# Attention and an ELU MLP on one core: the swapped copy of q by DMA, exp(h) - 1 on ScalarE, and q, k and the last weights of a pair handled at other half slots

## The chip, the cores and the metric

The kernel runs on one core of one Trainium2 chip. The metric is device time in microseconds of one execution; lower is better. Three runs of the kernel before gave 1304.9, 1305.69 and 1305.71 us, so the median is 1305.69 us. The engines are named as in the profile: PE (TensorE), ACT (ScalarE), DVE (VectorE), POOL (GpSimd) and SP, whose queue issues every DMA of this kernel.

## What is computed

The reference is RMS-normalised attention for 8 batches of 12 heads (448 positions, 64 wide), then an MLP whose activation is ELU with alpha = 1:

```python
q_n, k_n = rmsnorm(q, g_q), rmsnorm(k, g_k)
scores = (1 / np.sqrt(64)) * q_n @ k_n.transpose(0, 1, 3, 2)
attn = np.exp(scores - max) ; attn = attn / (sum(attn) + 1e-9)
x = (attn @ v) -> (8 * 448, 768)
h = x @ w_in                                  # 768 -> 2048
g = np.where(h > 0, h, np.exp(np.minimum(h, 0)) - 1)
out = g @ w_out                               # 2048 -> 768
```

Matmuls run on float16 parts: every operand is split into a high and a low float16 part, and a product of two operands is three matmuls (high by high, high by low, low by high) that add up in PSUM. For q and k, the high and the low part of one head share the 128 partitions.

## The kernel before, in words

**Tiles.** Two heads form a pair `p` (48 pairs, 6 per batch). The scores of a pair are 896 rows of 448, handled as 7 chunks `T` of 128 rows; `T % NJ` (NJ = 7) is the chunk's place in its pair. The MLP of a batch is 16 groups `f` of 18 matmuls (the m1 part, `w_in`, tile `mo`) and then 6 groups `d` of 48 matmuls (the m2 part, `w_out`).

**Half slots.** The order on every engine is written out by hand. One loop runs over half slots `h`; two half slots are one chunk and 14 are one pair. In each half slot the loop records the chunk's steps, then the tasks that `at(h, fn)` has put down for `h`, then a share of the MLP's matmuls (576 per 84 half slots, from h = 92 on), then the scores of the next chunk. Engines run their own instructions in this order, each waiting only for the data and the buffers that it needs.

**A chunk.** `s_mm` makes the scores on PE into one of four PSUM banks `s`. `s_max` (DVE) takes the row maximum, `s_exp` (ACT) the exponential and its sum, `s_z` (POOL) adds 1e-9, `s_rec` (DVE) takes the reciprocal, `s_hi` (ACT) writes the high part of the weights, `s_lo` (DVE) the low part, after which the bank is free. `s_tr` transposes both parts by a DMA into the tiles `pt` of the two heads. In chunk numbers: `s_max` of T stands at h = 2T, `s_exp` at 2T + 1, `s_z` and `s_rec` at 2T + 2 and 2T + 3, `s_hi` and `s_lo` at 2T + 4 and 2T + 5, and `s_tr` at 2T + 6 (2T + 8 for the first chunk of a pair, since its tile `pt` is free only after `attend` of the pair before).

**A pair.** `attend(p)` (22 matmuls on PE into the bank `av`) stands at h = 14(p + 1) + 7, and `x_high` (ACT) and `x_low` (DVE) bring its result into the MLP's input. Ahead of a pair, with hb = 14(p - 1), its q and k are prepared: `load_qk`, `qk_square` (ACT), `qk_sum` (DVE), `qk_root` (ACT), `qk_newton` (DVE), `qk_norm` (POOL, line 391), `k_high` (ACT), `q_gain` (POOL for pairs 1 to 6, otherwise DVE, line 405), `q_high` (ACT), `k_low` and `q_low` (POOL, lines 414 and 421), the two `qk_transpose` (DMAs, line 429) and `q_swap` (line 436). `q_swap` writes a copy of the transposed q whose two halves of 64 partitions have changed places; `s_mm` needs it for the second of its two matmuls, so that low parts meet high parts.

**The first batch.** Up to h = 92 there is attention alone on PE; beside it run the conversion of `w_in` (16 slabs, `conv_in`, with `s_high` on POOL at line 282) and later of `w_out` (24 slabs, `conv_out`, POOL at lines 313 and 322). From h = 92 on the MLP of one batch runs beside the attention of the next one. For v, POOL does `v_mult`, `v_high`, `v_low` and `v_shift` (lines 440, 448, 453, 459).

**A group of m1.** `m1_out` has five steps, one per half slot after the group's last matmul: exp(h) on ACT (line 614), minus 1 and times a power of two on POOL (617), the choice between that and h on DVE (623), and the high and low parts of g on ACT (628) and DVE (631).

Of the kernel before, what the change touches and what calls it, by code (L numbers as in the profile page):

```python
# [13 lines left out]
AF = mybir.ActivationFunctionType  # L14
ALU = mybir.AluOpType
# [7 lines left out]
NC_, NF = DM // 128, DFF // 128  # L23
NJ = 2 * S // 128
# [8 lines left out]
def tile_attention_then_elu_mlp(ctx: ExitStack, tc: tile.TileContext, qk, v, v_scan, gg, w_in, w_out, out):  # L33
# [13 lines left out]
    nc = tc.nc  # L47
# [15 lines left out]
    def t_mo():  # L63
# [8 lines left out]
        out=neg, in0=ident, scalar1=-1.0, scalar2=None, op0=ALU.mult  # L72
# [43 lines left out]
    def small(name, w=1, dt=F32, bufs=2):  # L116
        return pool.tile([128, w], dt, tag=name, name=name, bufs=bufs)
# [19 lines left out]
    def ibits(dst, src, s1, op0, s2, op1):  # L137
        nc.vector.tensor_scalar(
            out=dst.bitcast(I32), in0=src.bitcast(I32), scalar1=s1, scalar2=s2, op0=op0, op1=op1
        )  # L140
# [195 lines left out]
    vscale, mscale, vpow = {}, {}, {}  # L336
# [96 lines left out]
    def q_swap(p):  # L433
        q = qkt[p]
        for a, z in ((64, 0), (0, 64)):
            nc.gpsimd.tensor_copy(out=q[z : z + 64, 2], in_=q[a : a + 64, 0])  # L436

    def v_mult(p):
        n = vn[p]
# [49 lines left out]
    def m_scale(b):  # L489

        p2 = vpow[b]
        if b == 0:
            ibits(a_in, a_in, POWER, ALU.bitwise_and, 0, ALU.bitwise_or)
        am = small("am")
        nc.vector.tensor_reduce(out=am, in_=a_in, axis=AX.X, op=ALU.max)
        sc, isc = small("sc", NF), small("isc", NF)
        gsc = small("gsc", NF)
        nc.vector.tensor_scalar(  # L500
            out=sc, in0=a_in, scalar1=p2, scalar2=2.0 ** (-28 - UP), op0=ALU.mult, op1=ALU.mult
        )
        ibits(isc, sc, -1, ALU.mult, 254 * E, ALU.add)

        u = small("u", bufs=3)
        nc.vector.tensor_scalar(
            out=u, in0=am, scalar1=p2, scalar2=2.0 ** (-12 - UP), op0=ALU.mult, op1=ALU.mult
        )
        ui = small("ui")
        ibits(ui, u, -1, ALU.mult, 254 * E, ALU.add)  # L510
        nc.vector.tensor_scalar(out=gsc, in0=sc, scalar1=ui, scalar2=None, op0=ALU.mult)
        mscale[b] = [sc, isc, gsc, u]

    def cuts(j):

# [50 lines left out]
    def s_lo(T):  # L566

        p16, ps, r = p16s[T], pss.pop(T), stats.pop(T)[:, 2:3]
        nc.vector.scalar_tensor_tensor(  # L569
            out=p16[:, S:], in0=ps[:, :S], scalar=r, in1=p16[:, :S], op0=ALU.mult, op1=ALU.subtract  # L570
        )
# [32 lines left out]

    def m1_out(b, f, ph):

        sc, isc, gsc = (t[:, f : f + 1] for t in mscale[b][:3])
        e = None
        g = gts[f]

        def one():
            nonlocal e
            e = pool.tile([128, S], F32, tag="e", name="e", bufs=3)
            nc.scalar.activation(e, ph[:, :S], AF.Exp, scale=sc)  # L614

        def two():
            nc.gpsimd.tensor_scalar(  # L617
                out=e, in0=e, scalar1=-1.0, scalar2=isc, op0=ALU.add, op1=ALU.mult
            )

        def three():

            nc.vector.scalar_tensor_tensor(  # L623
                out=e, in0=e, scalar=0.0, in1=ph[:, :S], op0=ALU.min, op1=ALU.max
            )

        def four():
            nc.scalar.activation(g[:, 0], e, AF.Copy, scale=gsc)  # L628

        def five():  # L630
            nc.vector.scalar_tensor_tensor(  # L631
                out=g[:, 1], in0=e, scalar=gsc, in1=g[:, 0], op0=ALU.mult, op1=ALU.subtract
            )

        return [one, two, three, four, five]

    def m2_out(b, d, py):
        u = mscale[b][3]
        y = ua = None

        def one():
            nonlocal ua
            ua = small("ua")
            nc.gpsimd.tensor_scalar(
                out=ua, in0=u, scalar1=a_out[:, d : d + 1], scalar2=2.0**-14, op0=ALU.mult,
                op1=ALU.mult,
            )

        def two():
            nonlocal y  # L650
            y = pool.tile([128, S], F32, tag="e", name="y", bufs=3)
            nc.scalar.activation(y, py[:, :S], AF.Copy, scale=ua)

        def three():
            nc.sync.dma_start(out=out[d * 128 : (d + 1) * 128, b * S : (b + 1) * S], in_=y)

        return [one, two, three]
# [43 lines left out]
    def at(h, fn, *args):  # L701
        tasks.setdefault(h, []).append((fn, args))
# [15 lines left out]
    }  # L718
    for p in range(NP):
        hb = HP * (p - 1)  # L720
        steps = (-20, -12, -10, -8, -6, -2, 1, 1, 3, 6, 4)
        steps = early.get(p) or [hb + h for h in steps]
        for h, fn in zip(steps, (
            load_qk, qk_square, qk_sum, qk_root, qk_newton, qk_norm, k_high, q_gain, q_high, k_low,
            q_low,
        )):

            at(-3 if p == 2 and fn == load_qk else h, fn, p)
        for h, i in ((6, 0), (8, 1)):
            at(hb + h, qk_transpose, p, i)  # L730
        at(hb + (10 if p else 11), q_swap, p)
        h0 = HP * p
        for h, fn in ((-2, load_v), (9, v_mult), (10, v_high), (11, v_low), (12, v_shift)):
            at(h0 + h + (5 if (p == 0) == (h > 0) and p < 2 else 0), fn, p)
        at(h0 + 22, x_high, p)
        at(h0 + 23, x_low, p)
# [30 lines left out]
    for h in range(H0, LAST):  # L767
        T, odd = divmod(h, 2)
        run_tasks(h, 0)
        ok = lambda t: 0 <= t < NCHUNK  # L770
        if odd:
            if ok(T):
                s_exp(T)
            if ok(T - 1):
                s_rec(T - 1)
            if ok(T - 2):
                s_lo(T - 2)
        else:
            if ok(T):
                s_max(T)  # L780
            if ok(T - 1):
                s_z(T - 1)
            if ok(T - 2):
                s_hi(T - 2)

            for t in (T - 4, T - 3):
                if ok(t) and (t % NJ == 0) == (t == T - 4):
                    s_tr(t)
        run_tasks(h, 1)
        want = int(max(0, (h + 1 - START)) * RATE)  # L790
        n = max(0, want - done)
        mm = []
        p, r = divmod(h, HP)

        if ok(T + 1) and odd == (h >= START):
            mm.append(lambda: s_mm(T + 1))
        if r == 7 and 0 <= p - 1 < NP:
            mm = [lambda mm=mm: (*(fn() for fn in mm), attend(p - 1))]
        parts = len(mm) + 1
        for k in range(parts):  # L800
            for _ in range(n * (k + 1) // parts - n * k // parts):
                r = next(moe, None)
                done += 1
                if r:
                    steps_at(h + 1, enumerate(r))
            if k < len(mm):
                mm[k]()
        run_tasks(h, 2)
# [50 lines left out]
```

## Time and profile before

| what | before |
|---|---|
| median of 3 runs | 1305.69 us |
| the profiled execution | 1306.18 us |
| its span, first to last instruction | 1304.4 us (1.8 us lie around it) |
| PE busy | 1192.3 us (91%) |
| DVE busy | 875.1 us (67%) |
| ACT busy | 800.5 us (61%) |
| POOL busy | 719.4 us (55%) |
| DMA packets' time, share of 16 engines | 71.4% |
| first matmul of the MLP | at 189.1 us |

Times inside the span are counted from its first instruction. Busy time on PE is modelled from the starts of pipelined matmuls. A row of the waits reads: who waited, for whom, the total in us, how often, the longest. A row of the windows reads: the stretch, its length, then per engine the busy us and the number of instructions, then the granted TensorE clock, the DMA engines' busy share and GB/s. A row of the timeline reads: start, duration, engine, line, operation, what it writes and reads, how often, and in brackets the idle time of the engine before it with what ended it; SPq rows are DMA issues on SP's queue.

### The profile page before, as it was taken

To read this page: it belongs to the slowest core of one execution; us is meant where nothing else is said; L and a number is where in the kernel's file an instruction comes from. 1 tells how busy PE (TensorE), PEld (TensorE's weight loads), DVE (VectorE), ACT (ScalarE), POOL (GpSimd) and SP (SyncE) were. 2 spreads that over 40 slices of the span, in tenths; PEclk is the share of its full clock that TensorE was granted. 3 is DMA by queue.
4 is the path that set the end of the run, shared out by engine and by line. 5 is a ranking of instruction groups with operands and counts; after the bars stand their busy time and mean duration, and the time that the engine had idled before them with its cause. 6 is when DMAs were issued, how large, how long until landed. Compare 5 with 4: busy or idle time off the path is not lost.

```text
span 1304.4 us, 21596 instructions
## 1 busy us (share of the span) xinstructions
PE 1192.3 (91%) x6976; PEld 716.9 (55%) x6976; DVE 875.1 (67%) x1905; ACT 800.5 (61%) x1761; POOL 719.4 (55%) x1067
## 2 busy tenths in 40 slices
PE   2666558899999999999999999999999999999998
PEld 1323224456655775567556665576556655666576
DVE  6878898987578566866687558756686668642310
ACT  5777777776577566765677457655675467643310
POOL 4676678886465545655566456654665456531100
PEclk9786679999999999999999999999999999999999
DMA  7888887979877795769667986678677966764011
GB/s 251 199 190 209 192 204 180 204 177 202 181 133 147 171 215 128 156 138 238 135 136 151 201 169 133 143 183 199 130 150 146 230 135 148 137 124 107 1 47 61
DMA packets 444881, 208.22 MB, mean 160 GB/s; under 512 B 407136, under 2 KB 421088, under 8 KB 444768
## 3 DMA queue, kind: packets, MB, share of 16 engines
q1 hardware_dynamic: 444768, 206.85, 71.4%
q8 instruction: 55, 0.90, 0.3%
q14 instruction: 58, 0.48, 0.1%
HBM read 93.52 MB, written 14.16 MB: 83 GB/s over the span
## 4 chain that ended last, share of the span: by engine, by line
PE 71%; DMA 3%; DVE 1%; SPq 1%; issue 0%; ACT 0%; ACTq 0%
PE mo L676 29%; PE mo L690 28%; PE s L533 7%; PE av L590 6%; DMA pt<-p 2%; DMA vscan<-in_v_scan 1%; SPq L579 0%; DVE p L569 0%; DMA out<-y 0%; DVE st L540 0%; SPq L429 0%; DVE mv L167 0%; ACT p L564 0%; SPq L162 0%; SPq L665 0%
## 5 line engine op out<-in xcount | busy, mean ns | idle before, releaser
L676 PE MATMUL mo<-x,whi 128*128 128x448 f16 x1536 | 422.9, 353 | 5.7 <-DVE e L623 5.7
L690 PE MATMUL mo<-gall,whos 128*128 128x448 f16 x1536 | 423.0, 353 | 0.1
L540 DVE TENSOR_REDUCE st<-s 128x1 f32<-128x448 f32 x336 | 208.3, 620 | 188.5 <-PE s L533 186.8
L690 PE MATMUL mo<-gall,wls 128*128 128x448 f16 x768 | 272.1, 354 | 0.0
L676 PE MATMUL mo<-x,wli 128*128 128x448 f16 x768 | 271.0, 353 | 0.0
L564 ACT ACTIVATE p<-s,st 128x448 f16<-128x448 f32 x294 | 185.6, 631 | 133.5 <-DMA pt<-p 115.0
L690 PEld LDWEIGHTS <-whos 128*128 128x128 f16 x1536 | 221.6, 145 | 72.5
L546 ACT ACTIVATE s<-s,st 128x448 f32<-128x448 f32 x336 | 203.5, 606 | 87.5 <-DVE st L540 87.3
L550 POOL TENSOR_SCALAR st<-st 128x1 f32<-128x1 f32 x336 | 80.4, 239 | 304.0 <-ACT s L546 283.1
L533 PE MATMUL s<-qkt 128*128 128x448 f16 (+1 forms) x768 | 190.9, 371 | 59.4 <-DVE gall L569 37.9
L676 PEld LDWEIGHTS <-whi 128*128 128x128 f16 x1536 | 150.0, 98 | 144.2 <-issue 7.9
L569 DVE SCALAR_TENSOR_TENSOR p<-s,st,p 128x448 f16<-128x448 f32 x294 | 197.0, 670 | 29.0 <-ACT p L564 27.7
L617 POOL TENSOR_SCALAR e<-e,isc 128x448 f32<-128x448 f32 x128 | 95.2, 743 | 149.8 <-ACT e L614 147.8
L533 PEld LDWEIGHTS <-qkt 128*128 128x128 f16 (+1 forms) x768 | 63.2, 102 | 130.5 <-issue 72.0
L690 PEld LDWEIGHTS <-wls 128*128 128x128 f16 x768 | 110.6, 144 | 42.2 <-issue 7.8
L631 DVE SCALAR_TENSOR_TENSOR gall<-e,gsc,gall 128x448 f16<-128x448 f32 x128 | 104.5, 817 | 23.0 <-ACT gall L628 23.0
L628 ACT ACTIVATE gall<-e,gsc 128x448 f16<-128x448 f32 x128 | 85.4, 667 | 52.3 <-DVE e L623 52.1
L590 PE MATMUL av<-pt,vt 128*64 128x448 f16 x1056 | 112.1, 358 | 5.1 <-DMA pt<-p 5.1
L676 PEld LDWEIGHTS <-wli 128*128 128x128 f16 x768 | 75.0, 98 | 74.7 <-issue 7.5
L623 DVE SCALAR_TENSOR_TENSOR e<-e,mo 128x448 f32<-128x448 f32 x128 | 78.5, 613 | 35.4 <-POOL e L617 35.3
L614 ACT ACTIVATE e<-mo,sc 128x448 f32<-128x448 f32 x128 | 79.9, 624 | 31.2 <-PE mo L676 31.2
L436 POOL COPY qkt<-qkt 64x896 f16<-64x896 f16 x96 | 93.5, 974 | 5.0
(100 smaller groups left out, 1409.8 us busy)
## 6 DMA issues: line engine op xcount, KB each, us to landing
wls<-wl_d SPq DMA_DIRECT2D x48, 512.0 KB, 4.2
nat<-in_qk SPq DMA_DIRECT2D x48, 448.0 KB, 3.7
raws<-in_w_out SPq DMA_DIRECT2D x24, 512.0 KB, 4.2
out<-y SPq DMA_DIRECT2D x48, 224.0 KB, 3.6
vn<-in_v SPq DMA_DIRECT2D x38, 256.0 KB, 3.5
vscan<-in_v_scan SPq DMA_DIRECT2D x36, 224.0 KB, 4.0
whos<-in_w_in SPq DMA_DIRECT2D x10, 768.0 KB, 5.3
pt<-p SPq DMA_TRANSPOSE x336, 3.2
```

What stands on the lines that cost most here:

```text
L436: nc.gpsimd.tensor_copy(out=q[z : z + 64, 2], in_=q[a : a + 64, 0])
L533: nc.tensor.matmul(ps[r0 : r0 + n, :S], lhs, qq[:, 1, h * S : h * S + S], start=(t == 0), stop=(t == 2),)
L540: nc.vector.tensor_reduce(out=st[:, 0:1], in_=pss[T][:, :S], axis=AX.X, op=ALU.max, negate=True)
L546: nc.scalar.activation(ps, ps, AF.Exp, bias=st[:, 0:1], accum_out=st[:, 1:2])
L564: nc.scalar.activation(p16[:, :S], pss[T][:, :S], AF.Copy, scale=stats[T][:, 2:3])
L569: nc.vector.scalar_tensor_tensor(out=p16[:, S:], in0=ps[:, :S], scalar=r, in1=p16[:, :S], op0=ALU.mult, op1=ALU.subtract)
L590: nc.tensor.matmul(av[64 * h : 64 * h + 64, :S], vt[p][:, j + NJ * i, h], pt[h][:, j, :], start=(k == 0), stop=(k == len(terms) - 1),)
L617: nc.gpsimd.tensor_scalar(out=e, in0=e, scalar1=-1.0, scalar2=isc, op0=ALU.add, op1=ALU.mult)
L628: nc.scalar.activation(g[:, 0], e, AF.Copy, scale=gsc)
L631: nc.vector.scalar_tensor_tensor(out=g[:, 1], in0=e, scalar=gsc, in1=g[:, 0], op0=ALU.mult, op1=ALU.subtract)
L676: nc.tensor.matmul(ph[:, :S], w[:, c, :], x[:, r, :], start=(c == 0 and i == 0), stop=last)
L690: nc.tensor.matmul(py[:, :S], w, g[:, r, :], start=(f == 0 and i == 0), stop=last)
```

## The change

It has four parts. `q_swap` becomes two DMAs on SP's queue in place of two POOL copies. The second step of `m1_out` becomes one ACT activation (Identity, with the power of two as scale and its negative as bias, one new small DVE instruction per batch) in place of the POOL operation. For pairs from 2 on, all preparation steps of q and k but the load, and the two transposes, stand two half slots sooner; `q_swap` stands at hb + 8 in place of hb + 10 (hb + 11 for pair 0). The last chunk of a pair is transposed right after its `s_lo`, one half slot sooner.

```diff
     def q_swap(p):
         q = qkt[p]
         for a, z in ((64, 0), (0, 64)):
-            nc.gpsimd.tensor_copy(out=q[z : z + 64, 2], in_=q[a : a + 64, 0])
+            nc.sync.dma_start(out=q[z : z + 64, 2], in_=q[a : a + 64, 0])
...
         ibits(isc, sc, -1, ALU.mult, 254 * E, ALU.add)
+        nisc = small("nisc", NF)
+        nc.vector.tensor_scalar(out=nisc, in0=isc, scalar1=-1.0, scalar2=None, op0=ALU.mult)
...
         def two():
-            nc.gpsimd.tensor_scalar(
-                out=e, in0=e, scalar1=-1.0, scalar2=isc, op0=ALU.add, op1=ALU.mult
-            )
+            nc.scalar.activation(e, e, AF.Identity, scale=isc, bias=nisc)
...
-        steps = (-20, -12, -10, -8, -6, -2, 1, 1, 3, 6, 4)
+        steps = (-20, -14, -12, -10, -8, -4, -1, -1, 1, 4, 2)
...
-        for h, i in ((6, 0), (8, 1)):
+        for h, i in ((4 if p > 1 else 6, 0), (6 if p > 1 else 8, 1)):
             at(hb + h, qk_transpose, p, i)
-        at(hb + (10 if p else 11), q_swap, p)
+        at(hb + 8, q_swap, p)
...
             if ok(T - 2):
                 s_lo(T - 2)
+                if T % NJ == 1:
+                    s_tr(T - 2)
...
             for t in (T - 4, T - 3):
-                if ok(t) and (t % NJ == 0) == (t == T - 4):
+                if ok(t) and t % NJ != NJ - 1 and (t % NJ == 0) == (t == T - 4):
                     s_tr(t)
```

Three places show what this does to the order. The first is POOL at the border of two pairs in the first batch, before: L448 and L453 are v_high and v_low, L436 the swap, L550 is `s_z`, L459 is v_shift, L391 is `qk_norm` of the next pair, L282 belongs to a slab of w_in and L405 is `q_gain`.

```order
L448 TENSOR_SCALAR vt<-gall 128x512
L436 COPY qkt<-qkt 64x896 x2
L453 TENSOR_TENSOR vt<-gall,vt 128x512
L550 TENSOR_SCALAR st<-st 128x1
L459 COPY vt<-vt 64x384 x2
L391 TENSOR_TENSOR nat<-nat,r_811 128x896
L282 TENSOR_SCALAR whi_98<-w32s,ws 128x768
L550 TENSOR_SCALAR st<-st 128x1
```

The same place in the changed kernel (`s_z` is L552 there):

```order
L448 TENSOR_SCALAR vt<-gall 128x512
L391 TENSOR_TENSOR nat<-nat,r_796 128x896
L453 TENSOR_TENSOR vt<-gall,vt 128x512
L552 TENSOR_SCALAR st<-st 128x1
L459 COPY vt<-vt 64x384 x2
L405 TENSOR_TENSOR nat<-nat,gst 128x448
L282 TENSOR_SCALAR whi_98<-w32s,ws 128x768
L552 TENSOR_SCALAR st<-st 128x1 x2
```

`qk_norm` of the next pair has moved to where the swap stood, ahead of the first `s_z`, and `q_gain` to where `qk_norm` stood.

The second place is SP's queue at a border of two pairs, before. L579 are the transposes of weights into `pt`; the two rows into pt_1361 wait for `attend` to free that tile. L429 transposes q and k of the pair that comes next.

```order
L579 DMA_TRANSPOSE pt_1183<-gall_130 128x7x128
L429 DMA_TRANSPOSE qkt_1251<-t16_1221 128x7x128
L216 DMA raws_131<-in_w_out 128x1024
L340 DMA nat_1355<-in_qk 128x896
L579 DMA_TRANSPOSE pt_1361<-gall_130 128x7x128 x2
L429 DMA_TRANSPOSE qkt_1251<-t16_1221 128x7x128
L579 DMA_TRANSPOSE pt_1361<-gall_130 128x7x128
```

And in the changed kernel, where L581 is the weights' transpose and L436 the swap:

```order
L581 DMA_TRANSPOSE pt_1184<-gall_130 128x7x128 x2
L216 DMA raws_131<-in_w_out 128x1024
L429 DMA_TRANSPOSE qkt_1217<-t16_1200 128x7x128 x2
L216 DMA raws_131<-in_w_out 128x1024
L340 DMA nat_1360<-in_qk 128x896
L581 DMA_TRANSPOSE pt_1366<-gall_130 128x7x128 x2
L436 DMA qkt_1217<-qkt_1217 64x896 x2
L581 DMA_TRANSPOSE pt_1366<-gall_130 128x7x128
```

The transpose of k now stands ahead of the rows that wait for `attend`, and the two swapping DMAs have taken its place behind them.

The third place is ACT in an m1 part, before: L614 and L628 are steps one and four of `m1_out`, L564 is `s_hi`, L546 `s_exp`, L370 and L371 are `qk_root`.

```order
L614 ACTIVATE e<-mo,sc 128x448
L564 ACTIVATE p_6231<-s,st 128x448
L628 ACTIVATE gall<-e,gsc 128x448
L546 ACTIVATE s,st<-s,st 128x448
L564 ACTIVATE p_6265<-s,st 128x448
L370 ACTIVATE ln<-ss,eps 128x14
L371 ACTIVATE r_6270<-ln 128x14
L628 ACTIVATE gall<-e,gsc 128x448
```

And in the changed kernel, where L616 and L629 are steps one and four, L620 is the new step two, and L566 and L548 are `s_hi` and `s_exp`:

```order
L616 ACTIVATE e<-mo,sc 128x448
L566 ACTIVATE p_6205<-s,st 128x448
L620 ACTIVATE e<-e,nisc,isc 128x448
L548 ACTIVATE s,st<-s,st 128x448
L616 ACTIVATE e<-mo,sc 128x448
L566 ACTIVATE p_6241<-s,st 128x448
L370 ACTIVATE ln<-ss,eps 128x14
L371 ACTIVATE r_6246<-ln 128x14
L629 ACTIVATE gall<-e,gsc 128x448
L620 ACTIVATE e<-e,nisc,isc 128x448
```

One activation more per group stands in the same in-order queue as the softmax of the next batch.

More of the change, by code (lines that the diff above doesn't have):

```diff
@@ L511, in m_scale @@
         nc.vector.tensor_scalar(out=gsc, in0=sc, scalar1=ui, scalar2=None, op0=ALU.mult)
-        mscale[b] = [sc, isc, gsc, u]
+        mscale[b] = [sc, isc, nisc, gsc, u]
     def cuts(j):
@@ L605, in m1_out @@
     def m1_out(b, f, ph):
-        sc, isc, gsc = (t[:, f : f + 1] for t in mscale[b][:3])
+        sc, isc, nisc, gsc = (t[:, f : f + 1] for t in mscale[b][:4])
         e = None
@@ L637, in m2_out @@
     def m2_out(b, d, py):
-        u = mscale[b][3]
+        u = mscale[b][4]
         y = ua = None
```

## The prediction

> **What bounds the kernel now.** I read the busy times by window first, then the waits of PE behind the start of its full load, then the waits and the timeline of the first batch, then the groups for prices.
>
> ```profile
> 60.00:189.00 129.00, 75.53 (x479) 37.02 (x477) 106.01 (x222) 94.83 (x211) 89.60 (x114) 0.72 0.82 200
> 189.10:277.50 88.40, 75.33 (x513) 38.59 (x512) 80.41 (x162) 67.66 (x145) 73.23 (x89) 1.00 0.81 186
> 774.60:844.00 69.40, 69.40 (x404) 35.69 (x403) 53.68 (x114) 49.95 (x111) 44.65 (x66) 1.00 0.67 140
> 355.00:1191.60 836.60, 833.16 (x4828) 507.60 (x4827) 566.02 (x1258) 526.26 (x1181) 462.90 (x731) 1.00 0.75 158
> ...
> PE av L590 <- DMA pt<-p: 3.4, 3, 1.9
> ```
>
> The kernel has two regimes. From 355 us on PE is busy 833.16 of 836.60 us at full clock, and the last row shows all the waits it has there: 3.4 us, in front of `attend`. What other engines gain there is worth nothing, unless they were late for PE; what they lose costs nothing until they are. Before 355 us PE is not the bound: from 60 to 189 us DVE works 106.01 of 129 us (82%), ACT 74%, POOL 69%, and from 189 to 277 DVE works 91%. No engine is full there; they wait for one another in the hand-written order:
>
> ```profile
> PE s L533 <- DMA qkt<-t: 11.0, 4, 4.3
> ...
> DVE st L557 <- POOL st L550: 12.1, 9, 2.5
> ```
>
> These are waits from 60 to 189 us: PE for the transpose of k, DVE for POOL's small `s_z`. Whatever ends the first regime sooner moves all behind it, since the MLP starts at a fixed half slot. So there are four terms: start, first batch, 189 to 355 us, and the full-PE part.
>
> **Prices.**
>
> ```profile
> L617 POOL TENSOR_SCALAR e<-e,isc 128x448 f32<-128x448 f32 x128 | 95.2, 743 | 149.8 <-ACT e L614 147.8
> L436 POOL COPY qkt<-qkt 64x896 f16<-64x896 f16 x96 | 93.5, 974 | 5.0
> L391 POOL TENSOR_TENSOR nat<-nat,r 128x896 f32<-128x896 f32 x47 | 81.7, 1739 | 9.6 <-issue 5.7
> ...
> L628 ACT ACTIVATE gall<-e,gsc 128x448 f16<-128x448 f32 x128 | 85.4, 667 | 52.3 <-DVE e L623 52.1
> ...
> L400 ACT ACTIVATE t<-nat 128x448 f16<-128x448 f32 x48 | 27.5, 572 | 3.8 <-POOL nat L391 3.8
> ...
> wl_d<-w32s SPq DMA_DIRECT2D x24, 128.0 KB, 2.1
> ...
> qkt<-t SPq DMA_TRANSPOSE x96, 3.1
> ```
>
> POOL loses 95.2 + 93.5 = 189 of its 719 us. ACT gains 128 activations that no row shows: SBUF to SBUF with two per-partition operands. L400 has none (572 ns), L628 one (667), so one operand costs 95 ns; the ends are 667 (the second is free) and 762, and I take 762 less the 0.1 us by which neighbours overlap, 0.66 us, thus 84 us in all. A swap moves 2 x 112 KB within SBUF; nearest is the 128 KB store, 2.1 us to landing, and as upper end a transpose, 3.1.
>
> **The start: -2 us (0 to -3.9).**
>
> ```profile
> 13.96 1.22 SPq L429 DMA_TRANSPOSE qkt<-t  x1
> ...
> 21.97 1.19 DVE L230 SCALAR_TENSOR_TENSOR wts<-wts,w32s 128x768 uint32<-128x768 uint32 x1 [1.44 <-ACT w32s L225]
> ...
> 22.41 0.56 PE L533 MATMUL s<-qkt 128*128 128x448 f16 x1 [4.68 <-POOL qkt L436]
> ...
> 24.60 0.49 ACT L293 ACTIVATE wli<-mo 128x384 f16<-128x384 f32 x1 [2.66 <-PE mo L290]
> ```
>
> The first scores wait 4.68 us for POOL's copies. By DMA, right behind the issue of k's transpose (13.96 to 15.2 us), they land about 15.2 + 0.5 + 2.1 to 3.1, near 18.5: 3.9 us sooner. DVE's weights up to 23.2 us hang on ACT, so the first maximum does not move; the slab matmuls behind the scores on PE do, and ACT waits 2.66 us for these. I take 2.
>
> **The first batch: -4 us (+2.5 to -6), five borders.** The tempting sum is that each of the five `s_z` waits behind a swap goes. The order says otherwise. One border, before:
>
> ```profile
> 66.12 1.29 SPq L429 DMA_TRANSPOSE qkt<-t  x1
> ...
> 66.42 1.90 POOL L436 COPY qkt<-qkt 64x896 f16<-64x896 f16 x2
> ...
> 68.41 1.16 POOL L453 TENSOR_TENSOR vt<-gall,vt 128x512 f16<-128x512 f32 x1
> ...
> 69.56 0.54 PE L533 MATMUL s<-qkt 128*128 128x448 f16 x2 [2.25 <-DMA qkt<-t]
> ...
> 69.87 0.16 DVE L557 RECIPROCAL st<-st 128x1 f32<-128x1 f32 x1 [2.23 <-POOL st L550]
> ...
> 71.03 2.27 POOL L391 TENSOR_TENSOR nat<-nat,r 128x896 f32<-128x896 f32 x1
> ...
> 73.29 1.60 POOL L282 TENSOR_SCALAR whi<-w32s,ws 128x768 f16<-128x768 f32 x1
> 74.94 0.48 PE L290 MATMUL mo<-whi,neg 128*128 128x384 f16 x1 [2.81 <-POOL whi L282]
> ...
> 75.19 0.16 DVE L557 RECIPROCAL st<-st 128x1 f32<-128x1 f32 x1 [1.07 <-POOL st L550]
> 75.23 1.13 POOL L405 TENSOR_TENSOR nat<-nat,gst 128x448 f32<-128x448 f32 x1
> ```
>
> The swap (1.90 us) leaves the place ahead of the first `s_z`, and `qk_norm` (1.74 in the mean, 2.27 here) takes it: that `s_z` moves by -0.2 to +0.4 us, and DVE's 2.23 us of waiting stays. Behind it, `q_gain` (1.13) stands where `qk_norm` (2.27) stood, so the slab and the second `s_z` come about 1.90 + 2.27 - 2.27 - 1.13 = 0.8 us sooner, 1.3 if `qk_norm` takes its mean; DVE's 1.07 and part of PE's 2.81 go. PE's first scores hung on the transpose of k, issued at 66.12 behind the two transposes that wait for `attend`, and went at 69.56. Now the swap stands at that place: second DMA issued about 66.6, landed at 68.7 (2.1 later) to 69.7 (3.1), so PE goes 0.9 us sooner to 0.1 later. Most of what the earlier transposes give is taken back by the DMA that must wait for q's transpose. Both paths together I put at -0.8 us a border (-1.2 to +0.5). That the last chunk is transposed sooner gives nothing here: PE does not wait for `pt` in this part.
>
> **189 to 355 us: -4 us (+4 to -8).**
>
> ```profile
> PE mo L676 <- DVE e L623: 5.7, 5, 2.1
> ...
> DVE e L623 <- POOL e L617: 2.8, 1, 2.8
> ...
> 189.10:355.00 165.90, 13.88 (x16) 1.00 0.85 190
> ...
> L631 DVE SCALAR_TENSOR_TENSOR gall<-e,gsc,gall x128: 668/684/1857, 205.6 to 1249.1; 128x448 f16<-128x448 f32 x128
> ...
> L569 DVE SCALAR_TENSOR_TENSOR p<-s,st,p x294: 653/666/685, 184.0 to 1181.4; 128x448 f16<-128x448 f32 x147
> ```
>
> Here DVE is nearest to full, and PE waits for it. Its 2.8 us for POOL's step two go. Its L631 takes 13.88 us for 16 (868 ns each; window of that line) against a median of 684: 3 us stretched while POOL works, of which half may go. With some `s_z` waits DVE gets some 5 us, PE perhaps 4. Against it: ACT takes 16 x 0.66 = 10.6 us more, 67.66 to 78.2 of 88.4 us (88%), which may take the 4 us back and cost 4 more; that is the upper end. The stretching is told in the Trainium skill, GPSIMD Engine Reference, section 1 (Specifications): POOL shares its SBUF interfaces with VectorE and collides with VectorE instructions that have two SBUF inputs or a two-port mode. The trace agrees: L569, which reads one operand from PSUM, never exceeds 685 ns, while L631, with two from SBUF, reaches 1857. By the rule only the lines of that kind are relieved; were all of DVE's work here relieved by POOL's share that goes (26%), this term would be nearer its end of -8.
>
> **The part with PE full: -1 us (+18 to -3.4).** The 3.4 us in front of `attend` hang on the last transposes, which are issued one half slot (about 1.65 us: 69.4 us for 42) sooner; the longest wait is 1.9, so nearly all go: -3. The swap here stands where the transpose of k stood, and five half slots remain until the scores. The risk is ACT in m1 parts:
>
> ```profile
> 784.50:796.00 11.50, 11.50 (x71) 5.96 (x71) 10.97 (x24) 10.14 (x23) 6.52 (x10) 1.00 0.51 111
> ...
> 805.33 0.67 DVE L569 SCALAR_TENSOR_TENSOR p<-s,st,p 128x448 f16<-128x448 f32 x1
> ...
> 808.50 0.54 PE L533 MATMUL s<-qkt 128*128 128x448 f16 x2
> ...
> ACT gall L628 <- DVE e L623: 4.5, 6, 2.2
> ACT p L564 <- DMA pt<-p: 4.4, 3, 3.1
> ACT s L546 <- DVE st L540: 2.9, 3, 1.5
> ```
>
> A whole m1 part goes from 49.95 to 60.5 of 69.40 us (87%). Its densest stretch, 784.5 to 796, has 1.36 us idle and gets 11.5 / 4.34 x 0.66 = 1.75: ACT falls 0.4 us behind and recovers later. PE has 2.5 us of cover: the bank that L569 frees at 806.0 is next written at 808.5. I cost it at 2 us for the 18 pairs of the six m1 parts; if the cover goes by a further 1 us a pair, 18.
>
> **Sum.** -2 - 4 - 4 - 3 + 2 = -11 us from the profiled execution's 1306.18 (span 1304.4 and 1.8 around it; 0.5 above the median of 1305.69): **1295 us**. The ends add up to 1285 and 1331.
>
> **The rivals.** *The gates only change hands.* The swap's landing replaces that of k's transpose, `qk_norm` replaces the swap, and DVE paces the first batch as before; only the waits for `attend` go, and ACT takes these back. For it: the order at the border, and DVE's 82 to 91%. Against it: POOL loses a quarter of its work, and the start hung on POOL. With -3 for `attend` and +2 for ACT it gives about 1305; I count all of 1303.6 to 1308.8 to it.
>
> *ACT sets the pace in m1 parts: slower.* Its place is ACT's queue behind `s_hi`, which waits for `pt` transposes at each border (4.4 us per part; the rows above are those of 774.6 to 844 us). Idle time that ends with PE shrinks when ACT is late, but that which ends with DVE or DMA need not: per part ACT waits 4.5 us for DVE at L628, 4.4 for DMA and 2.9 for DVE at L546. If all of it stays, a part takes 60.5 + 11.8 = 72.3 us, 2.9 over; six parts 17 us, and 4 lost in the part from 189 us, against 6 gained at the start and in the first batch: 1306.2 + 15, about 1321. It decides once ACT's work and these waits pass 69.4 us. For it: 0.6 us a group in a full in-order queue. Against it: POOL's step two was itself waited for (2.8 us above), and ACT's queue has the PE-ended waits to give.
>
> *POOL was worth more.* If POOL's lateness sets the first batch, DVE's whole 12.1 us behind `s_z` go, and the other lower ends hold: 1306.2 - 12.1 - 2 - 8 - 3.4 = 1281. The order at the border speaks against it, since `s_z` still stands behind `qk_norm`.
>
> **How the numbers follow.** Forecast 0.61 (1285 to 1303), gates change hands 0.18, ACT sets the pace 0.16 (1309 to 1330), POOL worth more 0.05. The range of 1284 to 1311 takes in the first two and the near end of the third. A measurement can tell 0.2% (2.6 us) from no change: faster 0.66, same 0.18, slower 0.16.
>
> **What would show it.** Start: PE's wait for the swap ends near 18.5 us. First batch: PE's waits at the borders name the swapping DMA in place of k's transpose, and are no shorter by more than 0.9 us; the first `s_z` still comes behind a 1.7 us POOL operation; the first MLP matmul comes at about 183 us, not 189.1. Later: no wait of PE for `pt`; ACT at 60 us per m1 part, PE still full there. I am wrong if m1 parts take over 70 us (ACT), if the new activation takes other than 0.67 to 0.76 us, or if the MLP's first matmul moves by less than 2 us or more than 10.

## The result, and the profile after

The changed kernel took 1286.95 us in the median of 4 runs (1285.78 to 1288.35), beside 1305.7 for the kernel before in the same rounds: a ratio of 0.985, 95% interval 0.984 to 0.986. The profiled execution took 1287.73 us with a span of 1285.6, against 1304.4: 18.8 us less, where the forecast said 11.

Windows of the kernel after, cut where the program's stages end as in the prediction's windows (the first MLP matmul comes at 178.8 us, the second batch's at 340.1). The columns are those of the prediction's first fence:

```profile
60.00:178.80 118.80, 72.79 (x440) 34.66 (x439) 95.03 (x217) 92.62 (x206) 80.47 (x102) 0.73 0.94 211
178.80:264.80 86.00, 74.74 (x513) 38.73 (x512) 76.15 (x163) 75.74 (x158) 54.00 (x67) 1.00 0.91 201
757.40:826.80 69.40, 69.40 (x404) 35.69 (x403) 52.85 (x114) 59.27 (x126) 26.40 (x45) 1.00 0.72 150
340.00:1172.60 832.60, 832.53 (x4830) 507.18 (x4829) 558.82 (x1264) 583.52 (x1277) 320.92 (x566) 1.00 0.82 169
```

The last row has PE busy for all but 0.07 us: the 3.4 us in front of `attend` are gone, and an m1 part takes 69.40 us as it did, with ACT at 59.27 of them. The first row is 118.8 us long where it was 129, and DVE is busy 95.03 us of it, before 106.01; since the changed kernel is a little further on at 60 us, the whole stretch from the start is compared below. The groups give the price of what was added:

```profile
L620 ACT ACTIVATE e<-e,nisc,isc 128x448 f32<-128x448 f32 x128 | 96.9, 757 | 0.3
...
qkt<-qkt SPq DMA_DIRECT2D x96, 112.0 KB, 2.4
```

By stages, the 18.8 us are: 3.1 up to the second pair's first row maximum (47.3 to 44.2 us; the first pair's stays at 23.1 to 23.2), 7.2 from there to the MLP's first matmul (189.1 to 178.8 in all), 4.7 in the first batch's MLP beside the next attention (166.0 to 161.3, up to the second batch's first matmul), 4.1 in the part with PE full (836.6 to 832.5, up to the last batch's first), and -0.3 in the tail.

### The profile page after: what moved, and what is told of

Read it like the earlier page. It is cut to its first block, busy times and chain, and to the rows that moved or that the text cites. A ratio compares the mean times of both kernels' runs of the same rounds, so it can differ in the third digit from the quotient of the medians.

```text
span 1285.6 us, 21501 instructions
## 1 busy us (share of the span) xinstructions
PE 1191.8 (93%) x6976; PEld 716.4 (56%) x6976; DVE 853.3 (66%) x1913; ACT 878.7 (68%) x1889; POOL 529.4 (41%) x843
## 4 chain that ended last, share of the span: by engine, by line
PE 79%; ACT 6%; DVE 5%; POOL 4%; issue 3%; DMA 2%; SPq 0%; ACTq 0%; POOLq 0%; DVEq 0%
PE mo L691 32%; PE mo L677 30%; PE s L535 8%; PE av L592 7%; DMA pt<-p 2%; PE mo L289 1%; ACT w32s L225 1%; ACT wts L224 1%; POOL nat L391 1%; ACT s L548 1%; POOL whi L282 1%; DVE wts L230 1%; DVE gall L571 1%; DVE st L542 1%; DVE gall L632 1%
## 5 line engine op out<-in xcount | busy, mean ns | idle before, releaser
L552 POOL TENSOR_SCALAR st<-st 128x1 f32<-128x1 f32 x336 | 77.3, 230 | 552.4 <-ACT s L548 544.5
L566 ACT ACTIVATE p<-s,st 128x448 f16<-128x448 f32 x294 | 185.6, 631 | 119.2 <-DMA pt<-p 99.9
L548 ACT ACTIVATE s<-s,st 128x448 f32<-128x448 f32 x336 | 203.2, 605 | 61.4 <-DVE st L542 58.4
L632 DVE SCALAR_TENSOR_TENSOR gall<-e,gsc,gall 128x448 f16<-128x448 f32 x128 | 100.8, 787 | 24.4 <-ACT gall L629 24.2
L629 ACT ACTIVATE gall<-e,gsc 128x448 f16<-128x448 f32 x128 | 85.1, 665 | 24.3 <-DVE e L624 24.3
L599 ACT ACTIVATE x<-av 128x448 f16<-128x448 f32 x48 | 26.1, 543 | 104.4 <-PE av L592 104.4
L620 ACT ACTIVATE e<-e,nisc,isc 128x448 f32<-128x448 f32 x128 | 96.9, 757 | 0.3
L616 ACT ACTIVATE e<-mo,sc 128x448 f32<-128x448 f32 x128 | 80.6, 630 | 22.3 <-PE mo L677 22.0
```

The lines of the kernel that those rows point to most:

```text
L548: nc.scalar.activation(ps, ps, AF.Exp, bias=st[:, 0:1], accum_out=st[:, 1:2])
L566: nc.scalar.activation(p16[:, :S], pss[T][:, :S], AF.Copy, scale=stats[T][:, 2:3])
L620: nc.scalar.activation(e, e, AF.Identity, scale=isc, bias=nisc)
L632: nc.vector.scalar_tensor_tensor(out=g[:, 1], in0=e, scalar=gsc, in1=g[:, 0], op0=ALU.mult, op1=ALU.subtract)
```

## The experiments

The table holds all runs; "DVE busy" is DVE's time up to the MLP's first matmul, taken as in the four window rows shown further down. Each ratio is against the kernel before, run in the same rounds as the kernel itself. All times are us, from one profiled execution, but for the ratios. The texts set down before each run weigh two theories of the first batch: W, that its time came from shorter waits at the borders of pairs, and S, that it came from DVE's operations with two inputs in SBUF being held up less by POOL.

| kernel | ratio to before (95%) | MLP's first matmul | DVE busy up to it | first batch's MLP | PE-full part |
|---|---|---|---|---|---|
| before | 1 | 189.1 | 151.8 | 166.0 | 836.6 |
| after | 0.985 (0.984 to 0.986) | 178.8 | 143.3 | 161.3 | 832.5 |
| a_swap | 1.000 (0.998 to 1.001) | 185.1 | 150.7 | 161.3 | 842.4 |
| a_act | 1.004 (1.002 to 1.005) | 193.2 | 151.7 | 168.6 | 836.4 |
| a_shift | 0.991 (0.988 to 0.993) | 184.0 | 145.5 | 163.0 | 832.7 |
| a_last | 0.996 (0.994 to 0.997) | 188.9 | 151.8 | 164.0 | 832.2 |
| n_swap | 0.990 (0.988 to 0.992) | 184.7 | 145.5 | 162.6 | 831.7 |
| n_act | 0.985 (0.983 to 0.987) | 178.0 | 143.6 | 161.6 | 832.5 |
| n_shift | 0.995 (0.994 to 0.997) | 186.9 | 151.1 | 163.0 | 837.7 |
| v_hb7 | 0.986 (0.984 to 0.987) | 179.2 | 142.8 | 162.2 | 831.7 |
| v_norm | 0.986 (0.985 to 0.988) | 179.4 | 145.8 | 163.0 | 833.1 |
| v_pool | 0.990 (0.988 to 0.991) | 181.6 | 144.9 | 164.9 | 834.6 |
| v_sooner | 0.983 (0.981 to 0.986) | 174.5 | 142.6 | 162.7 | 832.4 |
| v_null | 1.001 (1.000 to 1.003) | 190.8 | 153.1 | 165.6 | 836.3 |

### One part alone

Four kernels make one part of the change each, in the kernel before. **a_swap** (the transposes stay at hb + 6 and hb + 8; the swap stands at hb + 8, right behind that of k):

```diff
-            nc.gpsimd.tensor_copy(out=q[z : z + 64, 2], in_=q[a : a + 64, 0])
+            nc.sync.dma_start(out=q[z : z + 64, 2], in_=q[a : a + 64, 0])
...
-        at(hb + (10 if p else 11), q_swap, p)
+        at(hb + 8, q_swap, p)
```

> The kernel before with the swap by DMA alone, at hb + 8 right behind the transpose of k, which keeps its old place. Theory W (the time of the first batch came from waits): the start gains 3 us, but the swap now lands some 1.2 us after k's transpose did, so each of the five borders loses 1; the MLP's first matmul at 189 to 192 us, total 1304 to 1308. Theory S (it came from DVE's operations with two SBUF inputs, lines 230 and 256, being stretched less by POOL): without the copies DVE's busy time up to the MLP's start falls by 3 us or more, the first matmul at 184 to 187 us, total 1300 to 1303.

**a_act** (with the one small DVE instruction per batch that makes its bias, not shown):

```diff
-            nc.gpsimd.tensor_scalar(
-                out=e, in0=e, scalar1=-1.0, scalar2=isc, op0=ALU.add, op1=ALU.mult
-            )
+            nc.scalar.activation(e, e, AF.Identity, scale=isc, bias=nisc)
```

> The kernel before with step two of m1_out on ACT alone. The MLP's first matmul stays at 189 us under every theory, since no group of m1 ends before. W and S: the part from there to the end of the first batch's MLP (166 us) loses 2 to 4 us, the m1 parts stay at 69.4 us, total 1302 to 1304. Rival (ACT sets the pace): m1 parts over 70 us, total 1308 or more.

**a_shift** (the swap stays on POOL):

```diff
-        steps = (-20, -12, -10, -8, -6, -2, 1, 1, 3, 6, 4)
+        steps = (-20, -14, -12, -10, -8, -4, -1, -1, 1, 4, 2)
-        for h, i in ((6, 0), (8, 1)):
+        for h, i in ((4 if p > 1 else 6, 0), (6 if p > 1 else 8, 1)):
-        at(hb + (10 if p else 11), q_swap, p)
+        at(hb + (8 if p > 1 else 10 if p else 11), q_swap, p)
```

> The kernel before with q's and k's preparation and transposes two half slots sooner, the swap still two POOL copies, at hb + 8 for pairs from 2 on. No DMA stands behind attend for the scores any more. W: PE's 11 us of waiting for the transposes go and nothing takes their place: the first matmul of the MLP at 180 to 184 us, total 1297 to 1301. S: POOL does as much as before, DVE's busy time up to the MLP's start falls by under 2 us: 186 to 189 us, total 1303 to 1306.

**a_last**:

```diff
+                if T % NJ == 1:
+                    s_tr(T - 2)
-                if ok(t) and (t % NJ == 0) == (t == T - 4):
+                if ok(t) and t % NJ != NJ - 1 and (t % NJ == 0) == (t == T - 4):
```

> The kernel before with a pair's last weights transposed at once, alone. The first matmul of the MLP stays at 189 us; PE's waits for pt behind 355 us (3.4 us) go: total 1302 to 1303. Rival: the transpose only comes to stand in a fuller queue and the waits stay: 1305.5 to 1306.

The shift alone is worth 0.9%, the last chunk 0.45%, the swap nothing, and step two on ACT costs 0.35%. Neither theory came through these four runs whole. a_swap started the MLP when S said, but DVE's busy time fell by 1.1 us where S asked for 3 or more, and the total fits W. a_act's MLP started 4.1 us later, ahead of the first activation that was moved, and then the first batch's MLP took 2.6 us more where both theories had 2 to 4 less. a_shift took 6.3 us off DVE's time, where S forecast under 2, and its start of 184.0 us is W's upper end. For the later runs S therefore stands in another form: what counts is where `qk_norm` stands, not how much POOL does. a_last's 3.4 us of waits went as forecast, and its gain of about 6 us is larger.

a_swap's zero hides gains and a loss: in the profiled execution (1303.4 us, where the median of ten is 1306.9) its MLP starts 4.0 us sooner, the first batch's MLP takes 4.7 less, and then the PE-full part takes 5.8 more. PE's waits in a_swap from 340 to 1200 us name the place:

```profile
PE av L590 <- DMA pt<-p: 6.4, 4, 2.3
PE av L590 <- DMA vscan<-in_v_scan: 1.4, 1, 1.4
PE s L533 <- DMA qkt<-qkt: 0.9, 1, 0.9
```

They sum to 8.7 us where the kernel before had 3.4 from 355 us on. All end with DMAs, and most with the weights' transposes. One border of a_swap in SP's queue:

```profile
395.02 1.30 SPq L429 DMA_TRANSPOSE qkt<-t  x1
396.42 1.17 SPq L436 DMA_DIRECT2D qkt<-qkt  x2
397.69 1.30 SPq L579 DMA_TRANSPOSE pt<-p  x1
```

The two issues of the swap hold up the transpose behind them by 1.2 us, and the swap itself stands behind the late transpose of k; that this is the whole 5.8 us was not tried. In a_shift 0.6 us of these waits are left and in a_last none, so either part by itself does what the prediction gave to the last chunk. That the shift does it too, the prediction did not say.

### One part undone

**n_swap** is the changed kernel with the swap back on POOL (at hb + 8 for pairs from 2 on, for the first two where it was before), **n_act** with step two back on POOL (the removed lines of a_act's edit in place of the added one), **n_shift** with the old half slots:

```diff
-        steps = (-20, -14, -12, -10, -8, -4, -1, -1, 1, 4, 2)
+        steps = (-20, -12, -10, -8, -6, -2, 1, 1, 3, 6, 4)
-        for h, i in ((4 if p > 1 else 6, 0), (6 if p > 1 else 8, 1)):
+        for h, i in ((6, 0), (8, 1)):
```

> The changed kernel with the swap back on POOL (two copies, at hb + 8 for pairs from 2 on). W: PE's 9.0 us of waiting for the swapping DMA at the borders go, the start loses its 3 us again: the MLP's first matmul at 175 to 180 us against 178.8, total 1284 to 1288. S, as the first four runs have left it (DVE's stretched operations depend on where qk_norm stands, not on the copies, and DVE paces the first batch): the waits for the swap only become waits for score banks, the start is lost: 182 to 185 us, total 1290 to 1293.

> The changed kernel with step two of m1_out back on POOL. The first matmul of the MLP stays at 178.8 us, give or take the 4 us by which the first batch moved where nothing in it was changed. If taking the step off POOL pays (as forecast), the 161.3 us from there to the end of the first batch's MLP become 163.5 to 165.5, total 1289 to 1292; if ACT gives it all back, they stay or fall, total 1284 to 1287.5. The part with PE full stays at 832.5 us in both.

> The changed kernel without the shift: swap by DMA, step two on ACT and the last chunk at once are kept, q and k are prepared where they were. POOL is as idle as in the changed kernel. Theory S (DVE sets the pace of the first batch, and its operations on two SBUF operands are stretched by where POOL's large ones fall; the shift moved these away): DVE's busy time up to the MLP's first matmul stays near 150 us (before 151.8, changed 143.2), that matmul comes at 184 to 187 us, and the full-PE part stays near 837 to 842 us since the swap lands behind the late transpose of k; about 1302. If POOL's lighter load is what counted, the start comes near 179 us and the time near 1290.

n_act is within 0.8 us of the changed kernel in every column, though POOL is busy 630.3 us in it and 529.4 in the changed one: **moving step two to ACT buys nothing in the changed kernel**, neither beside the first batch's MLP (161.6 against 161.3) nor later. n_shift loses two thirds of the gain, although its POOL is as light: the MLP starts 8.1 us later, and the PE-full part takes 5.2 us more. Both lie within what S gave for it. n_swap loses one third: its MLP starts 5.9 us later, as S had it (182 to 185 us). So the swap by DMA needs the shift: without it the PE-full part is longer than before (842.4 and 837.7 us, before 836.6), with it shorter. What the last chunk is worth within the change was not tried.

### What the shift does to DVE

The windows of DVE alone from the start to the MLP's first matmul, for before, after, a_shift and n_shift:

```profile
0.00:189.10 189.10, 151.84 (x323) 0.77 0.82 208
```

```profile
0.00:178.80 178.80, 143.25 (x324) 0.79 0.93 226
```

```profile
0.00:184.00 184.00, 145.50 (x323) 0.78 0.87 214
```

```profile
0.00:186.90 186.90, 151.13 (x324) 0.77 0.90 220
```

DVE does the same 323 operations (and the change's own small one) in 8.6 us less. About 6.3 us of this go with the shift, not with the load taken off POOL: a_shift has them with the swap still on POOL, and n_shift has the changed kernel's load on POOL and the DVE time of the kernel before. The other 2.2 come with the swap off POOL once the shift is made (n_swap has 145.5 us). Which operations became shorter, the groups of DVE from 23 us to the MLP's first matmul show, before and after:

```profile
L256 DVE SCALAR_TENSOR_TENSOR w32s<-whos,wts 128x768 uint32<-128x768 uint32 x10 | 13.2, 1315 | 0.0
L256 DVE SCALAR_TENSOR_TENSOR w32s<-raws,wts 128x512 uint32<-128x512 uint32 (+1 forms) x12 | 11.3, 944 | 0.0
L378 DVE SCALAR_TENSOR_TENSOR r<-ss,r 128x14 f32<-128x14 f32 x7 | 3.3, 477 | 0.2
L381 DVE TENSOR_SCALAR r<-r,kap 128x7 f32<-128x7 f32 x7 | 2.4, 346 | 0.2
...
L138 DVE TENSOR_SCALAR a_in<-a_in 128x16 int32<-128x16 int32 x1 | 1.7, 1683 | 0.0
```

```profile
L256 DVE SCALAR_TENSOR_TENSOR w32s<-whos,wts 128x768 uint32<-128x768 uint32 x10 | 10.7, 1074 | 0.0
L256 DVE SCALAR_TENSOR_TENSOR w32s<-raws,wts 128x512 uint32<-128x512 uint32 (+1 forms) x12 | 9.5, 794 | 0.0
...
L381 DVE TENSOR_SCALAR r<-r,kap 128x7 f32<-128x7 f32 x7 | 1.6, 231 | 0.2
L378 DVE SCALAR_TENSOR_TENSOR r<-ss,r 128x14 f32<-128x14 f32 x7 | 1.2, 174 | 0.2
```

L256 (the sign step of the weights' conversion) gives 4.3 us, L378 and L381 (`qk_newton`, 14 and 7 elements a row) 2.9, and the one L138 of 1683 ns takes 156 after, 1.5 less: together 8.7, about the 8.6. The timeline shows what they met. First the same L256 at the border of pairs 1 and 2, with POOL's operations, before and after:

```profile
71.03 2.27 POOL L391 TENSOR_TENSOR nat<-nat,r 128x896 f32<-128x896 f32 x1
...
72.21 1.90 DVE L256 SCALAR_TENSOR_TENSOR w32s<-whos,wts 128x768 uint32<-128x768 uint32 x1
```

```profile
65.97 1.72 POOL L405 TENSOR_TENSOR nat<-nat,gst 128x448 f32<-128x448 f32 x1
...
67.15 1.35 DVE L256 SCALAR_TENSOR_TENSOR w32s<-whos,wts 128x768 uint32<-128x768 uint32 x1
```

Then an L378 of a later pair, before, and the same one after:

```profile
162.40 1.16 POOL L322 TENSOR_TENSOR w32s<-w32s,whos 128x512 f16<-128x512 f32 x1 [0.33 <-ACT whos L318]
162.55 1.04 DVE L378 SCALAR_TENSOR_TENSOR r<-ss,r 128x14 f32<-128x14 f32 x1
```

```profile
150.39 0.17 DVE L378 SCALAR_TENSOR_TENSOR r<-ss,r 128x14 f32<-128x14 f32 x1
```

POOL's `qk_norm` (L391) ends at 73.30 us and DVE's L256 0.81 us later; in the other kernel POOL's L405 ends at 67.69 and the same L256 again 0.81 us later, though the two overlapped for 1.09 us in the one and 0.54 in the other. The 14-element operation ends at 163.59, POOL's at 163.56. DVE's operation does not run at a lower rate: **it waits for the rest of POOL's operation**, and the trace books the wait as busy time. This is what the Trainium skill says in SBUF — State Buffer, section "SBUF: two separate sides": the port pair that VectorE and GpSimd share is an exclusive lock for a whole instruction, and the other one blocks. These rows agree.

It is the order of starting that decides, not POOL's number of inputs. In the changed kernel POOL's L282, which reads one tensor, starts at 57.20 us and holds up DVE's L230, which ends 0.81 us after it; at the border above DVE's L256 starts first, and it is L282 that takes 1.60 us in place of 0.90:

```profile
57.20 0.90 POOL L282 TENSOR_SCALAR whi<-w32s,ws 128x768 f16<-128x768 f32 x1 [1.38 <-DVE ws L138]
```

```profile
57.50 1.41 DVE L230 SCALAR_TENSOR_TENSOR wts<-wts,w32s 128x768 uint32<-128x768 uint32 x1 [0.40 <-ACT w32s L225]
```

```profile
67.68 1.60 POOL L282 TENSOR_SCALAR whi<-w32s,ws 128x768 f16<-128x768 f32 x1
```

In all fourteen traces, 305 operations of L230 and L256 between 20 us and the MLP's start took over 1.1 times the shortest of their width (940 ns at 768 columns, 680 at 512). Each of them met a POOL operation that was already running, and ended 0.80 to 0.82 us (768 columns) or 0.54 to 0.55 us (512) after that one's end.

### Do the gates at a border matter?

Theory W was that the first batch's gain came from shorter waits at the borders of pairs. Two kernels take such waits away from the changed kernel. **v_hb7** puts the swap's DMAs ahead of the transposes that wait for `attend`:

```diff
-        at(hb + 8, q_swap, p)
+        at(hb + (7 if p > 1 else 8), q_swap, p)
```

> The changed kernel with the swapping DMAs one half slot sooner (hb + 7), so that they stand ahead of the transposes that wait for attend. W: PE's waits for the swap (9.0 us up to the MLP's start, five of them) go: first matmul at 173 to 177 us, total 1281 to 1285. S: DVE paces the first batch, the waits go over into waits for score banks: 177.5 to 179 us, total 1285.5 to 1287.

**v_norm** puts `qk_norm` back by two half slots, behind `s_z`:

```diff
-        steps = (-20, -14, -12, -10, -8, -4, -1, -1, 1, 4, 2)
+        steps = (-20, -14, -12, -10, -8, -2, -1, -1, 1, 4, 2)
```

> The changed kernel with qk_norm alone two half slots later again (hb - 2), behind v_shift, so that nothing long stands ahead of the first s_z of a border. W: DVE's waits for s_z there (9.9 us up to the MLP's start) fall to 4 or less, first matmul at 173 to 177 us, total 1281 to 1285. S: qk_norm meets the weights' two-input operations on DVE (lines 230 and 256) again as before the change, DVE's busy time up to the MLP's start rises from 143.2 by 3 us or more and eats the gain: 178 to 183 us, total 1286 to 1291.

The waits from 23 to 179 us, first after, then v_hb7, then v_norm:

```profile
PE s L535 <- DVE gall L571: 39.3, 20, 4.0
...
DVE st L559 <- POOL st L552: 9.9, 7, 1.9
PE s L535 <- DMA qkt<-qkt: 9.0, 5, 2.3
```

```profile
PE s L535 <- DVE gall L571: 47.9, 22, 5.1
```

```profile
DVE st L559 <- POOL st L552: 3.4, 5, 1.1
```

In v_hb7 the row of the swap is gone, all 9.0 us of it, and PE's wait for DVE to free a bank grows by 8.6: the MLP starts 0.4 us later than in the changed kernel. In v_norm DVE's wait for `s_z` falls from 9.9 to 3.4 us, and its busy time rises from 143.3 to 145.8: the start is 0.6 us later. Both totals (1288.3 and 1289.4 us) lie over 3 us above W's range, v_hb7's 1.3 above S's and v_norm's within it. A wait that is taken away here comes back elsewhere, the sign that these waits do not set the pace. v_norm also says that DVE's busy time alone does not: 2.5 us more of it cost 0.6 us.

### POOL's time, or the path of the swap?

**v_pool** keeps the swap by DMA and has POOL copy into a tile that nobody reads:

```diff
         for a, z in ((64, 0), (0, 64)):
             nc.sync.dma_start(out=q[z : z + 64, 2], in_=q[a : a + 64, 0])
+        for a, z in ((64, 0), (0, 64), (64, 0)) if p > 1 else ():
+            nc.gpsimd.tensor_copy(out=spare[z : z + 64], in_=q[a : a + 64, 0, :5])
```

> The changed kernel with the swap by DMA, and for pairs from 2 on POOL copies to a spare tile as well, at the same place, about as long as its old swap (1.9 us), which nobody reads. With the swap on POOL the MLP's first matmul came at 184.7 us, with it by DMA at 178.8. If POOL's time is what the DMA saves (s_z behind it, the stretch of DVE), this run lies near 184 us and 1293; if it is the path from q's transpose to the scores, near 179 and 1287.

Copies that nobody waits for (2.1 us a pair, the swap on POOL 1.9) cost as much as the swap on POOL did: a ratio of 0.990 like n_swap's, and 8.3 us of span (2.8 up to the MLP's start, 3.6 in the first batch's MLP, 2.1 later). The MLP's start lies halfway between the two forecasts, and the parts of n_swap's 5.9 us say why: 3.7 of them are there at the second pair already (47.9 us against 44.2), where v_pool copies nothing, and 2.2 come behind it, less than v_pool's 2.8. So at the start the DMA's worth is the path from q's transpose to the scores; behind it the numbers fit the POOL time that it frees, though 2.2 and 2.8 us are within what single profiles differ by (see below). How much of it is DVE's stretch (143.3 to 144.9) and how much POOL's lateness (DVE's wait for `s_z` is 13.6 us in v_pool) was not separated.

### Sooner still, and a change that does nothing

**v_sooner** moves `qk_norm` and all behind it one half slot more; **v_null** is the kernel before with the negated scale computed and never read.

```diff
-        steps = (-20, -14, -12, -10, -8, -4, -1, -1, 1, 4, 2)
+        steps = (-20, -14, -12, -10, -8, -5, -2, -2, 0, 3, 1)
-        for h, i in ((4 if p > 1 else 6, 0), (6 if p > 1 else 8, 1)):
+        for h, i in ((3 if p > 1 else 6, 0), (5 if p > 1 else 8, 1)):
```

> The changed kernel with qk_norm and all behind it, up to the two transposes, one half slot sooner still. If sooner is what the shift bought, the MLP's first matmul comes at 177 to 178 us and the time at 1285 to 1286. By theory S it is the place that counts: DVE's busy time up to there changes from 143.2 us as the meetings with POOL fall out, by up to 4 us either way, and the start goes with it.

```diff
+        nisc = small("nisc", NF)
+        nc.vector.tensor_scalar(out=nisc, in0=isc, scalar1=-1.0, scalar2=None, op0=ALU.mult)
```

> The kernel before with one more DVE instruction per batch on 128x16 elements that nobody reads (the negated scale alone). It measures how far the first batch moves by itself: with step two on ACT alone the MLP's first matmul came 4.1 us later although the order up to there was the same but for this instruction. If that is the first batch's own wobble, this run lies anywhere between 189 and 193 us and 1305 to 1311; if step two on ACT did it, it lies at 189.1 and within 0.1% of before.

In its profiled execution (1284.47 us, next to the fastest of four) v_sooner starts the MLP 4.3 us sooner than the changed kernel, with DVE busy 142.6 us, so this time DVE's idle time fell (from 35.5 to 31.9 us), which theory S does not say. Its median of 1286.45 us is that of the changed kernel, and the ratios' intervals overlap: it is not shown to be faster. v_null is not told apart from before either, yet its MLP started 1.7 us later in the profile, and before itself ran from 1304.5 to 1311.0 us in those rounds. With a_act's 4.1 us, where one small DVE instruction near its end is all that the first batch has more, differences of up to four us in a single profile's first batch prove nothing by themselves. Those of the shift stand apart: DVE's busy time up to the MLP is 142.6 to 145.8 us in the eight kernels with it, and 150.7 to 153.1 in the six without; the MLP starts at 174.5 to 184.7 us in the eight and at 185.1 to 193.2 in the six.

## Why the prediction was right in sign and short in size

**The start (-2): -3.1, right in mechanism.** The swap's issue on SP and the scores that wait for it on PE, in the timeline of the changed kernel:

```profile
15.40 1.17 SPq L436 DMA_DIRECT2D qkt<-qkt  x2
```

```profile
18.61 0.53 PE L535 MATMUL s<-qkt 128*128 128x448 f16 x1 [0.62 <-DMA qkt<-qkt]
```

PE's wait for the swap ended at 18.6 us, forecast 18.5; the first maximum stayed at 23.2 us, and the second pair came 3.1 us sooner. Every kernel with the swap by DMA has that pair's first maximum at 43.6 to 45.0 us, every one without it at 47.3 to 48.6: this term belongs to the swap (with its earlier place in the order) alone.

**The first batch (-4, at the lowest -6): -7.2. This is the term that was mis-sized.** With the start it moved the MLP's first matmul by 10.3 us, to 178.8 where about 183 was forecast. The prediction called itself wrong if that were more than 10, so by its own sign it was. The border went as the prediction read it from the order. The timeline of that border, after, by engine:

```profile
61.71 1.69 POOL L391 TENSOR_TENSOR nat<-nat,r 128x896 f32<-128x896 f32 x1
...
64.59 0.19 POOL L552 TENSOR_SCALAR st<-st 128x1 f32<-128x1 f32 x1
```

```profile
64.69 0.35 PE L535 MATMUL s<-qkt 128*128 128x448 f16 x1 [1.81 <-DMA qkt<-qkt]
```

```profile
64.82 0.16 DVE L559 RECIPROCAL st<-st 128x1 f32<-128x1 f32 x1 [1.79 <-POOL st L552]
...
69.58 0.16 DVE L559 RECIPROCAL st<-st 128x1 f32<-128x1 f32 x1 [1.07 <-POOL st L552]
```

The swap's DMA stands where the transpose of k stood (1.81 us of waiting, before 2.25), `qk_norm` stands ahead of the first `s_z` (1.79, before 2.23), and the two reciprocals lie 4.76 us apart, before 5.32: 0.6 sooner where 0.8 was forecast. `q_gain` (L405) took 1.72 us there, not the 1.13 of the sum; DVE's L230 was running when it started (65.50 to 66.70 us). But the working counted waits only, and v_hb7 and v_norm show that these don't set the pace there. The prediction named DVE's lines with two SBUF inputs, and weighed their stretch for 189 to 355 us alone, by POOL's share of work; for the first batch it put the stretch at nothing, without a reason. The stretch depends on which operations meet and which starts first, and in the first batch the shift changed the meetings of `qk_newton` and `qk_norm`: DVE's busy time up to the MLP's start fell by 8.6 us of the 10.3 by which the start and the first batch moved. The rows above show the meetings; that they pass on to the start nearly in full is argued from the table, where n_shift, without the shift, has DVE's old time and of the start's 10.3 us only 2.2. It is not shown: v_norm's 2.5 us of DVE time passed on 0.6 us, no run changed the meetings without moving the preparation, and in the changed kernel the profile's chain of work that ended last runs from 50 to 178.8 us through POOL for 47.3 us, PE for 30.7 and DVE for 20.5. So POOL, which waits for DVE in the same meetings, may pass on as much; in the kernel before this chain does not reach back into the first batch, and the two can't be compared.

**189 to 355 us (-4): -4.7, right in size for the wrong reason.** The prediction took it from POOL's step two and stretch, less ACT's load. ACT's load came as said (75.74 of 86 us, 88%), but n_act shows that step two on POOL or ACT makes no difference there. Alone, the swap has 4.7 of it, the shift 3.0 and the last chunk 2.0, so they don't add up, and which of them is behind the 4.7 stays open.

**The PE-full part (-1, at the lowest -3.4): -4.1.** The -3 for `attend` was right: all 3.4 us of these waits went. The other 0.6 us are PE's own busy time (833.16 before, 832.53 after), which was not followed up. The 2 us that ACT was to cost did not come: the activation took 757 ns (762 forecast), ACT 59.27 us a part (60.5), and n_act has the same 832.5. So ACT never set the pace in m1 parts, against that rival.

**The rivals.** That the gates only change hands was right about the gates and wrong about the time, since DVE's own pace changed. That POOL is worth more, by DVE's whole wait for `s_z`, is not what happened: 9.9 of the 12.1 us are still there. Of the 18.8 us the terms missed 7.8: 1.1 at the start, 3.2 in the first batch, 0.7 beside the first MLP and 3.1 with PE full, less 0.3 in the tail. The time of 1286.95 us came out inside the forecast's 1285 to 1303, near its lower end, and there luck had a part: two of the four terms fell below their own ranges, and a third was right for the wrong reason.

## What to carry to other kernels

Where DVE and POOL share a stage, look in the timeline for operations of either that take longer than their group's shortest, and see what the other runs at that moment: here the one that started first was let finish, and the wait is booked as busy time. Changing who meets whom can be worth more than taking work off POOL: the shift by two half slots gave 0.9% alone, the swap's removal from POOL nothing alone. A wait at a gate is worth its length only where no engine behind it is the bound: the 9.0 us taken away by v_hb7 came back as 8.6 for the banks. A part that gains nothing alone (the swap: 8.7 us won up to the second batch's MLP and 5.8 lost behind) can gain with another (the shift), so undo parts as well as making them alone.

## What the runs showed of the hardware

DVE's `qk_newton` on 14 elements a row took 1.04 us instead of 0.17 beside a POOL operation and ended 0.03 us after it. One L138 with a single tensor input (16 elements a row) took 1683 ns beside `qk_norm` (173.58 to 175.27 us) and ended 0.03 us after it, so two inputs are not the whole condition.

A copy of 112 KB within SBUF by a DMA landed in 2.4 us, near the 2.1 of a 128 KB store in the kernel before (3.2 for the same store after).

The MLP's start differs between kernels whose first batch has the same order. The same matmuls at the same place, in before and in a_act, whose orders are the same up to there:

```profile
42.43 0.89 PE L289 MATMUL mo<-w32s,dgw 128*128 128x384 f32 x2
```

```profile
43.49 1.63 PE L289 MATMUL mo<-w32s,dgw 128*128 128x384 f32 x2
```

Two matmuls took 1.63 us in place of 0.89. The granted clock from 36 to 47 us was 0.94 in before and 0.74 in a_act, with 49 matmuls in both; a_act's MLP started 4.1 us later. What lowered the clock was not found, nor whether this is all of a_act's 4.1 us.
